# Linear attention and gated MLP layers, prompt kernel: x^T k of the second attention layer by seven block products in place of eight

## The chip, the cores and the metric

The kernel runs on one core of one Trainium2 chip. The metric is the device time of one launch in microseconds (us). Before the change the median of three runs is 1485.83 us (1485.26 to 1486.38). The profile is one execution, with its own time.

## What is computed

The reference applies four blocks to x (2048 tokens of 1024 features): attention, MLP, attention, MLP, each with a layer norm before it and its input added to its output.

```python
def _A_ref(x, wqkv, wo):            # 32 heads of 32
    qkv = (x @ wqkv) ...            # q, k, v per head
    phi = lambda t: jnp.where(t > 0, t + 1, jnp.exp(t)) + 1e-6
    pq, pk = phi(q), phi(k)
    kv = jnp.einsum("bhsd,bhse->bhde", pk, v)
    z = jnp.einsum("bhsd->bhd", pk)
    num = jnp.einsum("bhqd,bhde->bhqe", pq, kv)
    den = jnp.einsum("bhqd,bhd->bhq", pq, z)[..., None] + 1e-6
    return (num / den) ... @ wo

def _B_ref(x, w_gate, w_up, w_down):
    return ((x @ w_gate) * (x @ w_up)) @ w_down
```

## The kernel before, in words

All tokens stay in SBUF as 16 tiles of 128 (X). One program runs layer_A(0), layer_B(1), layer_A(2), layer_B(3). The order of all instructions of each engine is the order in which the program issues them; nothing is reordered later, and each engine takes its own queue in order.

The kernel never forms v. Since kv = pk^T (x wv) = (x^T pk)^T wv, an attention layer computes XK = x^T pk (1024 x 1024) and multiplies it with wv (kv_unit, L662). "x" is here the normed input, xn_a: 16 tiles of 128 tokens x 1024 features, lying in TX, ST and the tails of K6 and K7. The phi-keys are 16 tiles, pk2 in the second layer (f16), in the tails of K0 to K5. The key sums z come from adding the 16 key tiles (sk, f32), splitting the total into two bf16 parts (z_parts, L446: one ScalarE copy, one VectorE subtraction), adding over the tokens with a product with ones (z_unit, L454), and turning the result into a column (z_column, L465).

The second attention layer, where the change is:

- The keys are computed in key_stage (L580), four groups of 512 tokens, each by seven block products for eight (key_product, L546; 8 matmuls of 512 columns each). Group u's products 1, 2, 6, 5, 7 are woven with products 4 and 3 of group u-1. Products 1, 6 and 7 are snapshot from PSUM by ScalarE (key_snap, L556); VectorE adds the snapshots to other products (key_add, L560, the add at L563; block 21 is read by ScalarE at L565). For each of the four blocks (11, 12, 21, 22) there follow exp on ScalarE (key_exp, L569) and three VectorE operations (key_max, L575 and L577). A block 'ln' is token parity l and feature half n. VectorE also forms the block sums of the x operand (key_sums, L534).
- PSUM is eight banks, used as four pairs QP[0] to QP[3]; in this layer key_stage takes them in the order QP3, QP1, QP0, QP2 (R).
- XK in eight pairs (xk_pair, L420): two blocks of 128 rows by 512 columns in one PSUM pair, 16 matmuls each (one for each token tile), and one ScalarE copy to XK (L435). The first pair begins inside key_stage, the last three are spread between the q tiles. XK lies in the heads of K5 and K4, where wk was.
- The key sums: 15 VectorE additions in f32 (sum_unit, L438 to L441), two before product 7 of the last group, two and four in the last round, and the rest while the first pairs run.
- q tiles (q_tile, L472): 16 matmuls (L404), phi by two ScalarE and two VectorE operations (L387, L391, L392, L394), then, some tiles later, through a list that is flushed in twos (L489), the division by the denominator (den_sums, L507; den_divide, L515) and a transposing DMA on SyncE's queue (tx, L340). 11 q tiles stand between the XK pairs, the last five behind kv_unit.
- Queues: SyncE's carries the transposes and the weight loads (load_qkv, L148; wq in the last round of key_stage, wv right behind key_stage). ScalarE's carries wo (load_o, L152). GpSimd's carries, in this stage, only the small norm statistics of tiles 12 to 15 (L296 to L331), woven into the first two rounds (key_norms, L653; KEY_FILL, L651). In the first attention layer GpSimd's queue also issues plain loads (scan_fetch, L223).

Of the kernel before, what the change touches and what calls it, by code (L numbers as in the profile page):

```python
# [38 lines left out]
def kernel(  # L39
# [11 lines left out]
    nc = tc.nc  # L51
    P = 128
# [30 lines left out]
    QQ = psum.tile([P, 8, NB], F32, tag="Q", name="Q")  # L83
    Q = [QQ[:, i, :] for i in range(8)]
    QP = [QQ[:, 2 * i:2 * i + 2, :] for i in range(4)]
    WD = dram.tile([7, P, BLK], F16, name="WD")

    HEAD = KD * NB
# [38 lines left out]
    SS = [K[1][:, i * D:(i + 1) * D].bitcast(F16).rearrange("p (k m s) -> p k m s", k=KH, m=2) for i in range(4)]  # L127
    TK = [W[:, 2 * i * D:2 * (i + 1) * D].bitcast(F16).rearrange("p (k n) -> p k n", n=NB) for i in range(3)]
    yk = [MX[:, i * D:(i + 1) * D].bitcast(F16).rearrange("p (m s) -> p m s", s=NB) for i in range(4)]
    ek = [b[:, i * D:(i + 1) * D].rearrange("p (m s) -> p m s", s=NB) for b in (K[7], K[1]) for i in range(4)]  # L130
    count = {}

    def turn(name, bufs):
        count[name] = count.get(name, -1) + 1
        return bufs[count[name] % len(bufs)]
# [281 lines left out]
            proj_mm(t, wk[n], ps[:, n, :])  # L417
        return ps, pk[t]

    def xk_pair(c, pk, order):  # L420

        n, j = divmod(2 * c, KD)
        bank = []

        def part(ts):
            if not bank:
                bank.append(mm_pair())
            for i in range(2):
                for t in ts:
                    nc.tensor.matmul(out=bank[0][:, i, :], lhsT=xn_a[t][:, (j + i) * P:(j + i + 1) * P],  # L430
                                     rhs=pk[t][:, n * NB:(n + 1) * NB], start=(t == order[0]), stop=(t == order[-1]))

        def end():
            part(order[-2:])
            nc.scalar.copy(out=XK[n][:, j:j + 2, :], in_=bank[0])  # L435
        return [lambda: part(order[:-2]), end]

    def sum_unit(t, eng, pk):  # L438

        def run():  # L440
            eng.tensor_tensor(out=sk, in0=pk[0] if t == 1 else sk, in1=pk[t], op=ALU.add)  # L441
        return run

    zparts = []
# [27 lines left out]
    def q_tile(t, split, mid=[], end=[], ring=4, done=2):  # L472

        while count.get("mm", -1) // 2 + 1 & 3 >= ring:
            mm_pair()
        ps = mm_pair()
        proj_mm(t, wq[0], ps[:, 0, :])
        do(mid)
        proj_mm(t, wq[1], ps[:, 1, :])
        do(end)  # L480
        pq = turn("pq", pqb)
        phi(ps, pq, split)
        for _ in range(done):
            flush()
        later.extend(over_den(t, pq))
# [60 lines left out]
    def key_product(u, p, pair):  # L546
        a11, a12, a21, a22 = key_blocks(u)
        st = {1: a11, 2: a12, 4: a22, 5: SS[0], 6: SS[1], 7: SS[2], 3: SS[3]}[p]
        for m in range(2):
            for k in range(KH):  # L550
                nc.tensor.matmul(out=pair[:, m, :], lhsT=st[:, k, m, :], rhs=kmove[p][:, k, :],  # L551
                                 start=(p in (1, 2, 5) and k == 0), stop=(k == KH - 1), skip_group_check=True)
# [1 line left out]
    kst = {}  # L554

    def key_snap(u, p, bank):  # L556
        kst[u, p] = turn("sk", SK)
        nc.scalar.activation(out=kst[u, p], in_=bank, func=ACT.Identity, bias=kq[:, 1:2])

    def key_add(u, b, sn, bank):  # L560
# [4 lines left out]
            nc.scalar.activation(out=kst[u, b], in_=bank, func=ACT.Identity, bias=kq[:, 1:2])  # L565

    def key_exp(u, b):
        e = turn("ek", ek[:4]) if u < NG - 1 or b == 11 else ek[4 + (22, 21, 12).index(b)]
        nc.scalar.activation(out=e, in_=kst[u, b], func=ACT.Exp, scale=kq[:, 0:1], bias=kq[:, 3:4])  # L569
        kst[u, b] = kst[u, b], e  # L570

# [5 lines left out]
            nc.vector.tensor_tensor(out=pk2[TPG * u + 2 * m + l][:, n * NB:(n + 1) * NB], in0=y[:, m, :],  # L577
                                    in1=e[:, m, :], op=ALU.max)

    def key_stage(R, fill, sks, xk):  # L580

        fill = list(fill)

        def fills(n):
            do(fill[:n])
            del fill[:n]

        fills(3)
        for u in range(NG + 1):
            a, b, c, a_, c_ = R[2 * u % 3], R[3], R[(2 * u + 1) % 3], R[(2 * u - 2) % 3], R[(2 * u - 1) % 3]  # L590
            now, was = u < NG, u > 0
            if now:
                key_product(u, 1, a)
                key_snap(u, 1, a)
            else:
                xk[0][0]()
            if was:
                key_exp(u - 1, 22)
                key_product(u - 1, 4, a_)
                key_add(u - 1, 21, 0, a_)  # L600
                key_exp(u - 1, 21)
                key_max(u - 1, 22)
                fills(KEY_FILL[u][0])
                if not now:
                    do(sks[:2])
                    del sks[:2]
            if now:
                key_product(u, 2, b)
                key_add(u, 11, 1, b)
            if was:  # L610
                key_max(u - 1, 21)
                if now:
                    key_exp(u, 11)
                key_product(u - 1, 3, c_)
# [12 lines left out]
            if now:  # L627
                key_product(u, 5, c)
            if was:
                key_max(u - 1, 12)  # L630
            else:
                key_max(u, 11)
            if not now:
                do(sks[:4])
                del sks[:4]
            if now:
                do(sks[:(0, 0, 0, 2)[u]])
                del sks[:(0, 0, 0, 2)[u]]
                if u == NG - 1:
                    load_qkv(wq, 0)  # L640
                key_product(u, 7, a)
                key_snap(u, 7, a)
                if u + 1 < NG:
                    key_sums(u + 1, (0, 1))
                key_add(u, 22, 7, c)
                if u + 1 < NG:
                    key_sums(u + 1, (2,))
                fills(KEY_FILL[u][2])
        assert not fill

# [177 lines left out]
    def do(units):  # L828
        for u in units:
            u()  # L830
# [32 lines left out]
    SCAN_KEY = tuple(range(4, 12))  # L863

    def layer_A(li, R=None):
        keys = pk2 if li else pk
        sks = [sum_unit(t, nc.vector, keys) for t in range(1, NT)]
        first_A = li == 0
        order = [t for t in range(NT) if t not in (13, 15)] + [13, 15] if li else list(range(NT))
        xk = [xk_pair(c, keys, order) for c in range(KD)]  # L870

        def scans(n=1):
            if first_A:
# [79 lines left out]
        if li:  # L953
            count["mm"] = 1
        rest = [lambda x=x: do(x) for x in xk[first:]]
        XT_ = 11

        for t in range(XT_):
            pos = [-(-len(rest) * x // (XT_ - 1)) for x in (t, t + 1)]
            xks = rest[pos[0]:pos[1]]  # L960
            if t == XT_ - 2:
                do(xks)
                xks = []
                load_o()
            q_tile(t, li > 0, done=2 * ((t > 1 or first_A) and t < XT_ - 1))
            do(xks)
            if t == li // 2:
                z_unit()
            elif t == 2 + li // 2:
                z_column()  # L970
            elif first_A and t == 7:
                scale_sum(0, 2)
            elif first_A and t == 9:
                scale_pow(0, 2)
                scale_root(0, 2)
            elif first_A and t == 10:
# [269 lines left out]
```

## Time and profile before

| what | us |
|---|---|
| median of three runs | 1485.83 |
| the profiled execution's own time | 1486.08 |
| its span | 1484.3 |
| TensorE busy in the span | 1475.9 |
| VectorE busy | 1030.0 |
| ScalarE busy | 739.6 |
| GpSimd busy | 96.5 |
| second layer: first key product to kv product | 750.66 to 894.04 |
| first pair of x^T k to kv product | 796.45 to 894.04 |
| matmuls of x^T k, second layer | 256 |

A line of a timeline reads: start, length, engine, line of the code, operation, output <- input, shape, count; in brackets the idle time before it and who ended it. A line of the chain reads: start, length, what. "L404 x16" is sixteen matmuls of line 404. A matmul's record lasts 0.379 us, but the next one starts 0.216 us after it, so records overlap; VectorE's overlap a little too. A line of a window reads: its limits, its length, then busy time and number of operations of PE, PEld, DVE, ACT and POOL, the granted clock, the share of the DMA engines, and GB/s.

### The profile page before, as it was taken

The numbers are of one execution on the slowest core, as the hardware profiler recorded it, in microseconds if no ns is written. First come the engines' busy times: TensorE is split into PE (matmuls) and PEld (weight loads), VectorE is DVE, ScalarE is ACT, GpSimd is POOL, SyncE is SP. The second block draws the span as 40 slices with busy tenths as digits, with TensorE's granted clock in tenths as the row PEclk, the third lists the DMA queues.
The fourth block names the chain that finished last, engine by engine and source line by source line (L and its number), as shares of the span: only waits on it lengthen the run. The fifth ranks groups of instructions, "written<-read, shape, count | busy, mean of one in ns | idle before, by whom it ended". The sixth has DMA issues, their size and how long they took to land.

```text
span 1484.3 us, 17639 instructions
## 1 busy us (share of the span) xinstructions
PE 1475.9 (99%) x6965; PEld 672.7 (45%) x6965; DVE 1030.0 (69%) x1460; ACT 739.6 (50%) x696; POOL 96.5 (6%) x219
## 2 busy tenths in 40 slices
PE   9999999999999999999999999999999999999999
PEld 3444444444444444444444445444444444444444
DVE  7856788888775577767388567867776846777532
ACT  5887695777601366640185337545663015666200
POOL 2121121000000000001130000200000100000000
PEclk9999999999999999999999999999999999999999
DMA  7867857776656333336533024353332763333442
GB/s 213 202 201 196 252 135 186 210 205 203 214 176 176 85 85 86 88 126 188 174 57 113 16 45 112 70 129 86 86 86 104 235 171 93 86 85 86 154 166 84
DMA packets 269650, 202.73 MB, mean 137 GB/s; under 512 B 101760, under 2 KB 256896, under 8 KB 265984
## 3 DMA queue, kind: packets, MB, share of 16 engines
q1 hardware_dynamic: 261232, 182.61, 43.6%
q0 software_dynamic: 4032, 14.68, 3.0%
q10 hardware_dynamic: 4304, 4.33, 0.9%
q8 instruction: 54, 0.88, 0.2%
q14 instruction: 28, 0.23, 0.0%
HBM read 160.43 MB, written 17.04 MB: 120 GB/s over the span
## 4 chain that ended last, share of the span: by engine, by line
PE 87%; POOL 1%; ACT 0%; DVE 0%; issue 0%
PE Q L755 46%; PE Q L1065 22%; PE Q L689 7%; PE Q L404 5%; PE Q L430 4%; PE Q L551 3%; PE Q L679 0%; PE Q L669 0%; POOL va L329 0%; ACT K L324 0%; POOL rs L330 0%; POOL nm L325 0%; POOL of L331 0%; DVE X L1079 0%; DVE W L396 0%
## 5 line engine op out<-in xcount | busy, mean ns | idle before, releaser
L755 PEld LDWEIGHTS <-K 128*128 128x128 f16 x3136 | 306.8, 98 | 370.0
L755 PE MATMUL Q<-XT,K 128*128 128x512 bf16 (+1 forms) x1792 | 405.7, 379 | 0.0
L1065 PE MATMUL Q<-K,K 128*128 128x512 f16 (+2 forms) x1582 | 340.4, 377 | 0.0
L755 PE MATMUL Q<-TX,K 128*128 128x512 f16 x1344 | 308.4, 379 | 0.0
L717 ACT ACTIVATE K<-K,fac 128x2048 f16<-128x2048 bf16 x112 | 224.6, 2008 | 128.8 <-DMA K<-in_B_w_gate_dram 128.8
L1065 PEld LDWEIGHTS <-K 128*128 128x128 f16 x1582 | 154.3, 98 | 184.5
L720 DVE TENSOR_TENSOR K<-K 128x1024 f16<-128x1024 f16 (+1 forms) x244 | 156.9, 665 | 103.4 <-ACT K L717 101.5
L720 DVE TENSOR_TENSOR W<-MX,Q 128x1024 f16<-128x1024 f32 x88 | 107.3, 1220 | 38.5 <-PE Q L755 19.6
L775 ACT COPY MX<-Q 128x1024 f32<-128x1024 f32 x60 | 60.8, 1012 | 124.1 <-PE Q L755 111.1
L720 DVE TENSOR_TENSOR W<-W,Q 128x1024 f16<-128x1024 f32 x80 | 97.6, 1220 | 17.9 <-PE Q L755 13.6
L775 ACT COPY W<-Q 128x1024 f32<-128x1024 f32 x52 | 52.7, 1013 | 92.2 <-PE Q L755 79.5
L720 DVE TENSOR_TENSOR K<-K,K 128x512 f16<-128x512 f16 (+1 forms) x148 | 87.7, 597 | 4.2
L404 PE MATMUL Q<-K,K 128*128 128x512 bf16 x384 | 86.8, 379 | 1.9 <-DMA K<-K 1.0
L404 PE MATMUL Q<-K,XT 128*128 128x512 bf16 x384 | 85.7, 379 | 1.2 <-DMA XT<-ST 0.6
L759 DVE TENSOR_TENSOR K<-W 128x512 f16<-128x512 f16 x168 | 71.4, 425 | 5.8
L231 ACT ACTIVATE K<-K 128x2048 bf16<-128x2048 bf16 x37 | 70.3, 1906 | 1.6 <-DMA K<-in_B_w_down_dram 1.5
L392 DVE TENSOR_SCALAR W<-W 128x1024 bf16<-128x1024 bf16 (+1 forms) x52 | 20.5, 393 | 66.7 <-ACT W L387 66.6
L1079 DVE SCALAR_TENSOR_TENSOR W<-Q,kap,X 128x1024 f32<-128x1024 f32 x16 | 20.5, 1284 | 66.1 <-PE Q L1065 66.1
L772 ACT COPY MX<-Q 128x1024 f32<-128x1024 f32 x28 | 28.3, 1009 | 71.9 <-PE Q L755 71.9
L387 ACT ACTIVATE W<-Q 128x1024 bf16<-128x1024 f32 (+1 forms) x52 | 49.2, 950 | 29.3 <-PE Q L404 29.3
L290 DVE BATCH_NORM_STATS2 st<-X 128x6 f32<-128x512 bf16 x92 | 58.2, 673 | 2.6 <-DMA X<-in_A_x_dram 2.6
L404 PEld LDWEIGHTS <-K 128*128 128x128 bf16 x384 | 37.2, 98 | 47.4 <-DMA K<-K 2.6
(158 smaller groups left out, 1334.2 us busy)
## 6 DMA issues: line engine op xcount, KB each, us to landing
K<-WD SPq DMA_DIRECT2D x28, 1792.0 KB, 7.5
K<-in_B_w_gate_dram SPq DMA_DIRECT2D x70, 512.0 KB, 4.0
K<-in_B_w_up_dram SPq DMA_DIRECT2D x56, 512.0 KB, 5.2
K<-in_A_wqkv_dram SPq DMA_DIRECT2D x10, 1024.0 KB, 6.0
K<-in_B_w_down_dram POOLq DMA_DIRECT2D x12, 512.0 KB, 5.8
K<-in_B_w_up_dram POOLq DMA_DIRECT2D x11, 512.0 KB, 5.2
K<-in_B_w_down_dram SPq DMA_DIRECT2D x10, 512.0 KB, 5.3
WD<-K SPq DMA_DIRECT2D x10, 512.0 KB, 3.0
```

The source lines that it names most:

```text
L231: nc.scalar.activation(out=scan_buf[i], in_=scan_buf[i], func=ACT.Square, accum_out=acc[:, m, c:c + 1])
L290: nc.vector.bn_stats(out=stat[t][0][:, c, :], in_=X[:, t, c * NB:(c + 1) * NB])
L387: nc.scalar.activation(out=e, in_=ps, func=ACT.Exp)
L404: nc.tensor.matmul(out=ps, lhsT=xt[:, k, tl * P:(tl + 1) * P], rhs=w[:, k, :], start=(k == 0), stop=(k == KD - 1))
L430: nc.tensor.matmul(out=bank[0][:, i, :], lhsT=xn_a[t][:, (j + i) * P:(j + i + 1) * P], rhs=pk[t][:, n * NB:(n + 1) * NB], start=(t == orde ...
L689: nc.tensor.matmul(out=ps[:, n, :], lhsT=xT[t // TPG][:, c, tl * P:(tl + 1) * P].bitcast(F16), rhs=KVo[c][:, n, :], start=(c == 0), stop=( ...
L717: nc.scalar.activation(out=b.bitcast(F16), in_=b, func=ACT.Copy, scale=fac[:, m:m + 1])
L720: eng.tensor_tensor(out=o, in0=a, in1=b, op=op)
L755: nc.tensor.matmul(out=pair[:, m, :], lhsT=stationary(n, p, m, k), rhs=moving[p][:, k, :], start=(p in (1, 2, 5) and k == 0), stop=(k == K ...
L759: nc.vector.tensor_tensor(out=hA[i][:, u, :], in0=gu[:, 0, :], in1=gu[:, 1, :], op=ALU.mult)
L775: nc.scalar.copy(out=snaps[u, p], in_=a)
L1065: nc.tensor.matmul(out=ps_[:, lo:hi], lhsT=act[:, u, j * P:(j + 1) * P], rhs=w[:, u, lo:hi], start=(p in (1, 2, 5) and u == 0), stop=(u == ...
```

## The change

x^T pk of the second layer is seen as 2 x 2 blocks: the tokens by parity of their tile (eight pairs of tiles, 2i and 2i+1), the rows of x^T by feature half, the columns by feature half of the keys. It is computed by seven products of sums of blocks (x_product: for each of two column parts jp, 2 x 8 matmuls of 512 columns). Products 1, 6 and 7 are snapshot from PSUM (SN2), product 4's bank is copied to XK, and products 2, 5 and 3 are added to a snapshot (x_add, VectorE). The sums S (of x, in five operations for eight tile pairs) and T (of the keys, one operation for a pair) are made by VectorE, most of them in place.

The key sums no longer run on VectorE alone. GpSimd's queue copies the first four key tiles into four DRAM rows WZ (f16 to f32; a row of a partition is padded by 64 elements) and adds the next eight to them by accumulating DMAs, a group's four in the round after it. In the last round three more add the four rows into one. VectorE adds the last four tiles (key_total), and one DMA adds the DRAM row to that in SBUF; key_parts takes the place of z_parts. The loop over t in key_stage also runs in the first round, where its range is -4 to 0.

The order of products, sums and q tiles is written out in xq_stage. wv is loaded behind product 6's second part, into the buffers that SX and TY use until then. The buffers of pq are taken by a fixed list in this layer.

```diff
@@ -83,6 +83,7 @@
     QQ = psum.tile([P, 8, NB], F32, tag="Q", name="Q")
     Q = [QQ[:, i, :] for i in range(8)]
     QP = [QQ[:, 2 * i:2 * i + 2, :] for i in range(4)]
+    WZ = [dram.tile([P, D + 64], F32, name=f"WZ{i}")[:, 0:D] for i in range(4)]
     WD = dram.tile([7, P, BLK], F16, name="WD")
 
     HEAD = KD * NB
@@ -127,7 +128,11 @@
     SS = [K[1][:, i * D:(i + 1) * D].bitcast(F16).rearrange("p (k m s) -> p k m s", k=KH, m=2) for i in range(4)]
     TK = [W[:, 2 * i * D:2 * (i + 1) * D].bitcast(F16).rearrange("p (k n) -> p k n", n=NB) for i in range(3)]
     yk = [MX[:, i * D:(i + 1) * D].bitcast(F16).rearrange("p (m s) -> p m s", s=NB) for i in range(4)]
-    ek = [b[:, i * D:(i + 1) * D].rearrange("p (m s) -> p m s", s=NB) for b in (K[7], K[1]) for i in range(4)]
+    ek = [b[:, i * D:(i + 1) * D].rearrange("p (m s) -> p m s", s=NB) for b in (K[7], K[1], MX) for i in range(4)]
+    SX, TY = (K[i][:, 0:HEAD].bitcast(F16).rearrange("p (i n) -> p i n", n=NB) for i in (3, 1))
+    SN2 = [b.bitcast(F32).rearrange("p (m s) -> p m s", s=NB)
+           for b in (K[0][:, HEAD:HEAD + 2 * D], MX[:, 2 * D:4 * D], W[:, 0:2 * D], W[:, 2 * D:4 * D], K[4][:, 0:2 * D])]
+    sk2, zhi, zlo = MX[:, 2 * D:4 * D].bitcast(F32), W[:, 5 * D:6 * D], MX[:, D:2 * D]
     count = {}
 
     def turn(name, bufs):
...
@@ -554,7 +559,7 @@
     kst = {}
 
     def key_snap(u, p, bank):
-        kst[u, p] = turn("sk", SK)
+        kst[u, p] = SN2[0] if (u, p) == (NG - 1, 6) else turn("sk", SK)
         nc.scalar.activation(out=kst[u, p], in_=bank, func=ACT.Identity, bias=kq[:, 1:2])
 
     def key_add(u, b, sn, bank):
@@ -565,7 +570,7 @@
             nc.scalar.activation(out=kst[u, b], in_=bank, func=ACT.Identity, bias=kq[:, 1:2])
 
     def key_exp(u, b):
-        e = turn("ek", ek[:4]) if u < NG - 1 or b == 11 else ek[4 + (22, 21, 12).index(b)]
+        e = turn("ek", ek[:4]) if u < NG - 1 or b == 11 else ek[{22: 4, 21: 8, 12: 9}[b]]
         nc.scalar.activation(out=e, in_=kst[u, b], func=ACT.Exp, scale=kq[:, 0:1], bias=kq[:, 3:4])
         kst[u, b] = kst[u, b], e
 
@@ -577,7 +582,7 @@
             nc.vector.tensor_tensor(out=pk2[TPG * u + 2 * m + l][:, n * NB:(n + 1) * NB], in0=y[:, m, :],
                                     in1=e[:, m, :], op=ALU.max)
 
-    def key_stage(R, fill, sks, xk):
+    def key_stage(R, fill, xp):
 
         fill = list(fill)
 
@@ -592,18 +597,20 @@
             if now:
                 key_product(u, 1, a)
                 key_snap(u, 1, a)
-            else:
-                xk[0][0]()
             if was:
                 key_exp(u - 1, 22)
+                if not now:
+                    xp(1, 0, QP[0])
+                    xp(1, 1, QP[2])
                 key_product(u - 1, 4, a_)
                 key_add(u - 1, 21, 0, a_)
                 key_exp(u - 1, 21)
                 key_max(u - 1, 22)
                 fills(KEY_FILL[u][0])
                 if not now:
-                    do(sks[:2])
-                    del sks[:2]
+                    xsums("S2", XG)
+                    tsums("T2", range(4))
+                    tsums_last((4, 5), 1)
             if now:
                 key_product(u, 2, b)
                 key_add(u, 11, 1, b)
@@ -626,17 +633,16 @@
             fills(KEY_FILL[u][1])
             if now:
                 key_product(u, 5, c)
-            if was:
+            if was and now:
                 key_max(u - 1, 12)
-            else:
+            elif now:
                 key_max(u, 11)
-            if not now:
-                do(sks[:4])
-                del sks[:4]
             if now:
-                do(sks[:(0, 0, 0, 2)[u]])
-                del sks[:(0, 0, 0, 2)[u]]
+                for t in range(TPG * (u - 1), TPG * u if was else 0):
+                    nc.gpsimd.dma_start(out=WZ[t % 4], in_=pk2[t], **({"accum_op": ALU.add} if t > 3 else {}))
                 if u == NG - 1:
+                    for i, j in ((0, 1), (2, 3), (0, 2)):
+                        nc.gpsimd.dma_start(out=WZ[i], in_=WZ[j], accum_op=ALU.add)
                     load_qkv(wq, 0)
                 key_product(u, 7, a)
                 key_snap(u, 7, a)
@@ -645,6 +651,10 @@
                 key_add(u, 22, 7, c)
                 if u + 1 < NG:
                     key_sums(u + 1, (2,))
+                if u > 1:
+                    tsums("T3", range(2 * u - 4, 2 * u - 2))
+                if u:
+                    xsums("S3", XG[(0, 0, 1, 3)[u]:(0, 1, 3, 5)[u]])
                 fills(KEY_FILL[u][2])
         assert not fill
 
+    def xpart(i, l, h, n=1):
+        return [xn_a[2 * j + l][:, h * NB:(h + 1) * NB] for j in range(i, i + n)]
+    def xspan(i, l, h, n):
+        if n == 1:
+            return xpart(i, l, h)[0]
+        b = TX[:, 0:6 * D] if i == 0 else ST[:, 0:4 * D]
+        return b.rearrange("p (i l h s) -> p i l h s", l=2, h=2, s=NB)[:, :, l, h, :]
+    XG = ((0, 3), (3, 2), (5, 1), (6, 1), (7, 1))
+    def xsums(which, groups):
+        for i, n in groups:
+            a11, a12, a21, a22 = (xspan(i, l, h, n) for h, l in ((0, 0), (0, 1), (1, 0), (1, 1)))
+            s2 = SX[:, i:i + n, :] if n > 1 else SX[:, i, :]
+            o, a, b, op = {"S3": (a21.bitcast(F16), a11, a21, ALU.subtract), "S2": (s2, a22, a21.bitcast(F16), ALU.subtract),
+                           "S1": (a11.bitcast(F16), s2, a11, ALU.add), "S4": (a12.bitcast(F16), a12, s2, ALU.subtract)}[which]
+            nc.vector.tensor_tensor(out=o, in0=a, in1=b, op=op)
+    def tsums(which, pairs):
+        for i in pairs:
+            b11, b21, b12, b22 = (pk2[2 * i + l][:, n * NB:(n + 1) * NB] for n in range(2) for l in range(2))
+            t2 = TY[:, i, :]
+            o, a, b, op = {"T3": (b12, b22, b12, ALU.subtract), "T2": (t2, b12, b11, ALU.add),
+                           "T1": (b11, b22, t2, ALU.subtract), "T4": (b21, b21, t2, ALU.subtract)}[which]
+            nc.vector.tensor_tensor(out=o, in0=a, in1=b, op=op)
+    def tsums_last(pairs, at):
+        for i in pairs:
+            b11, b21, b12, b22 = (pk2[2 * i + l][:, n * NB:(n + 1) * NB] for n in range(2) for l in range(2))
+            t = MX[:, (2 * at + i % 2) * NB:(2 * at + i % 2 + 1) * NB].bitcast(F16)
+            nc.vector.tensor_tensor(out=t, in0=b12, in1=b11, op=ALU.subtract)
+            nc.vector.tensor_tensor(out=TY[:, i, :], in0=b22, in1=t, op=ALU.subtract)
+    xsnap = {}
+    def x_product(p, jp, pair):
+        def operands(i, c):
+            even, odd = xn_a[2 * i], xn_a[2 * i + 1]
+            ke, ko = pk2[2 * i], pk2[2 * i + 1]
+            st = {1: even, 2: odd, 4: odd[:, NB:], 6: SX[:, i, :], 5: even.bitcast(F16), 7: even[:, NB:].bitcast(F16),
+                  3: odd.bitcast(F16)}[p]
+            mv = {1: ke[:, 0:NB], 2: ko[:, 0:NB], 3: ko[:, NB:], 4: ko[:, 0:NB], 6: TY[:, i, :], 5: ke[:, 0:NB], 7: ke[:, NB:]}[p]
+            return st[:, c * P:(c + 1) * P], mv
+        for pairs in (range(6), range(6, 8)):
+            for m in range(2):
+                for i in pairs:
+                    st, mv = operands(i, 2 * jp + m)
+                    nc.tensor.matmul(out=pair[:, m, :], lhsT=st, rhs=mv, start=(p in (1, 2, 5) and i == 0),
+                                     stop=(i == 7), skip_group_check=True)
+        if p in (1, 6, 7):
+            xsnap[p, jp] = SN2[{1: 2 + jp, 6: 0, 7: 4 - 3 * jp}[p]]
+            nc.scalar.copy(out=xsnap[p, jp], in_=pair)
+        elif p == 4:
+            nc.scalar.copy(out=XK[0][:, KH + 2 * jp:KH + 2 * jp + 2, :], in_=pair)
+    def x_add(p, jp, pair):
+        n, c, sn = {2: (0, 0, 1), 5: (1, KH, 7), 3: (1, 0, 6)}[p]
+        nc.vector.tensor_tensor(out=XK[n][:, c + 2 * jp:c + 2 * jp + 2, :], in0=xsnap.pop((sn, jp)), in1=pair, op=ALU.add)
+    def key_total():
+        nc.vector.tensor_tensor(out=sk2, in0=pk2[12], in1=pk2[13], op=ALU.add)
+        for t in (14, 15):
+            nc.vector.tensor_tensor(out=sk2, in0=sk2, in1=pk2[t], op=ALU.add)
+        nc.gpsimd.dma_start(out=sk2, in_=WZ[0], accum_op=ALU.add)
+    def key_parts():
+        nc.scalar.copy(out=zhi, in_=sk2)
+        nc.vector.tensor_tensor(out=zlo, in0=sk2, in1=zhi, op=ALU.subtract)
+        zparts[:] = [zhi, zlo]
+    def at_pair(i):
+        count["mm"] = 2 * i - 1
+    def xq_stage():
+        def q(t, i, done):
+            at_pair(i)
+            q_tile(t, True, done=done)
+        x_product(2, 0, QP[3])
+        x_product(2, 1, QP[1])
+        x_add(2, 0, QP[3])
+        key_max(NG - 1, 12)
+        tsums_last((6, 7), 0)
+        x_add(2, 1, QP[1])
+        x_product(6, 0, QP[0])
+        key_total()
+        tsums("T3", (4, 5, 6, 7))
+        q(0, 1, 0)
+        x_product(7, 0, QP[0])
+        xsums("S1", XG)
+        tsums("T1", range(8))
+        q(1, 3, 0)
+        x_product(5, 0, QP[1])
+        tsums("T4", range(8))
+        key_parts()
+        x_add(5, 0, QP[1])
+        q(2, 3, 0)
+        x_product(4, 0, QP[0])
+        xsums("S4", XG)
+        at_pair(3)
+        z_unit()
+        x_product(3, 0, QP[1])
+        x_add(3, 0, QP[1])
+        q(3, 3, 4)
+        x_product(6, 1, QP[2])
+        load_qkv(wv, 2)
+        at_pair(0)
+        z_column()
+        q(4, 1, 2)
+        x_product(7, 1, QP[2])
+        q(5, 3, 2)
+        x_product(5, 1, QP[0])
+        x_add(5, 1, QP[0])
+        q(6, 1, 2)
+        x_product(4, 1, QP[2])
+        q(7, 3, 2)
+        x_product(3, 1, QP[0])
+        x_add(3, 1, QP[0])
+        load_o()
+        q(8, 1, 2)
+        q(9, 0, 2)
+        q(10, 2, 0)
+        at_pair(3)
...
             count["mm"] = 7
-            key_stage(R, key_norms(), sks, xk)
-            load_qkv(wv, 2)
-            count["mm"] = 5
+            key_stage(R, key_norms(), x_product)
             eps[0] = kq[:, 2:3]
-        first = 3 if first_A else 2
+            xq_stage()
+        first = 3 if first_A else 0
         for i in range(first):
-            if first_A:
-                do(xk[i])
-            elif i == 0:
-                do([xk[1][0], xk[0][1]])
-            else:
-                do(xk[1][1:])
-            do(sks[5 * i:5 * i + 5] if first_A or i == 0 else sks[5 * i:])
...
-        for t in range(XT_):
+        for t in range(XT_ if first_A else 0):
...
         kv_unit()
+        if not first_A:
+            at_pair(1)
```

More of the change, by code (lines that the diff above doesn't have):

```diff
@@ L418, in k_tile, with xk_pair @@
         return ps, pk[t]
-    def xk_pair(c, pk, order):
+    def xk_pair(c):
         n, j = divmod(2 * c, KD)
@@ L430, in part, with sum_unit @@
                     nc.tensor.matmul(out=bank[0][:, i, :], lhsT=xn_a[t][:, (j + i) * P:(j + i + 1) * P],
-                                     rhs=pk[t][:, n * NB:(n + 1) * NB], start=(t == order[0]), stop=(t == order[-1]))
+                                     rhs=pk[t][:, n * NB:(n + 1) * NB], start=(t == 0), stop=(t == NT - 1))
         def end():
-            part(order[-2:])
+            part(range(NT - 2, NT))
             nc.scalar.copy(out=XK[n][:, j:j + 2, :], in_=bank[0])
-        return [lambda: part(order[:-2]), end]
-    def sum_unit(t, eng, pk):
+        return [lambda: part(range(NT - 2)), end]
+    def sum_unit(t):
         def run():
-            eng.tensor_tensor(out=sk, in0=pk[0] if t == 1 else sk, in1=pk[t], op=ALU.add)
+            nc.vector.tensor_tensor(out=sk, in0=pk[0] if t == 1 else sk, in1=pk[t], op=ALU.add)
         return run
@@ L480, in q_tile @@
         do(end)
-        pq = turn("pq", pqb)
+        pq = turn("pq", pqb) if eps[0] == 1e-6 else pqb[t % 4 if t < 6 else (4, 5, 0, 1, 2, 3)[t % 6]]
         phi(ps, pq, split)
@@ L865, in layer_A @@
     def layer_A(li, R=None):
-        keys = pk2 if li else pk
-        sks = [sum_unit(t, nc.vector, keys) for t in range(1, NT)]
+        sks = [sum_unit(t) for t in range(1, NT)]
         first_A = li == 0
-        order = [t for t in range(NT) if t not in (13, 15)] + [13, 15] if li else list(range(NT))
-        xk = [xk_pair(c, keys, order) for c in range(KD)]
+        xk = [xk_pair(c) for c in range(KD)]
         def scans(n=1):
@@ L935, in layer_A @@
             count["mm"] = 7
-            key_stage(R, key_norms(), sks, xk)
-            load_qkv(wv, 2)
-            count["mm"] = 5
+            key_stage(R, key_norms(), x_product)
             eps[0] = kq[:, 2:3]
-        first = 3 if first_A else 2
+            xq_stage()
+        first = 3 if first_A else 0
         for i in range(first):
-            if first_A:
-                do(xk[i])
-            elif i == 0:
-                do([xk[1][0], xk[0][1]])
-            else:
-                do(xk[1][1:])
-            do(sks[5 * i:5 * i + 5] if first_A or i == 0 else sks[5 * i:])
+            do(xk[i])
+            do(sks[5 * i:5 * i + 5])
             if i == first - 1:
@@ L952, in layer_A @@
             scans(3)
-        if li:
-            count["mm"] = 1
         rest = [lambda x=x: do(x) for x in xk[first:]]
         XT_ = 11
-        for t in range(XT_):
+        for t in range(XT_ if first_A else 0):
             pos = [-(-len(rest) * x // (XT_ - 1)) for x in (t, t + 1)]
@@ L964, in layer_A @@
                 load_o()
-            q_tile(t, li > 0, done=2 * ((t > 1 or first_A) and t < XT_ - 1))
+            q_tile(t, False, done=2 * (t < XT_ - 1))
             do(xks)
-            if t == li // 2:
+            if t == 0:
                 z_unit()
-            elif t == 2 + li // 2:
+            elif t == 2:
                 z_column()
-            elif first_A and t == 7:
+            elif t == 7:
                 scale_sum(0, 2)
-            elif first_A and t == 9:
+            elif t == 9:
                 scale_pow(0, 2)
                 scale_root(0, 2)
-            elif first_A and t == 10:
+            elif t == 10:
                 scale_bits(0, 2)
```

## Prediction

> **What bounds the kernel now.** I read the chain that ended last first, then its pieces in order of time, then TensorE's waits.
>
> ```profile
> ## 4 chain that ended last, share of the span: by engine, by line
> PE 87%; POOL 1%; ACT 0%; DVE 0%; issue 0%
> ...
> ```
>
> ```profile
> 754.85 41.60 PE Q L551 x192
> 796.45 6.04 PE Q L430 x28
> 802.49 3.45 PE Q L551 x16
> 805.95 7.77 PE Q L430 x36
> 813.72 3.45 PE Q L404 x16
> ...
> 894.21 3.57 PE Q L669 x64
> ```
>
> ```profile
> PE Q L551 <- ACT K L558: 0.6, 1, 0.6
> ```
>
> TensorE carries the end, and from 754.85 us, through the second layer's key stage and x^T k to the kv product, it never stops: the one wait of the key stage (0.6 us) ends where that chain begins. So a matmul removed here is worth its whole pitch, as long as no operand or bank comes late. Then VectorE, ScalarE and the GpSimd issues, because they get the new work:
>
> ```profile
> 788.55 0.55 DVE L575 TENSOR_SCALAR K<-K,fac,kq 128x1024 bf16<-128x1024 bf16 x1 [0.71 <-ACT K L569]
> 789.13 0.76 DVE L577 TENSOR_TENSOR K<-MX,K 128x512 f16<-128x512 f16 x2
> 789.81 1.21 DVE L563 TENSOR_TENSOR MX<-W,Q 128x1024 f16<-128x1024 f32 x1
> ...
> 811.78 13.82 DVE L441 TENSOR_TENSOR K<-K,K 128x1024 f32<-128x1024 f32 x11
> ```
>
> ```profile
> 754.00:796.00 42.00, 41.43 (x193) 18.67 (x191) 36.84 (x65) 34.78 (x33) 4.46 (x11) 1.00 0.17 36
> 796.00:894.00 98.00, 98.00 (x463) 44.51 (x461) 62.06 (x81) 35.88 (x35) 0.00 (x0) 1.00 0.26 74
> ```
>
> ```profile
> q0 software_dynamic: 4032, 14.68, 3.0%
> ```
>
> ```profile
> L223 POOL DMA_DIRECT2D K<-in_B_w_up_dram x11: 748/748/971, 87.3 to 120.0; - x11
> ...
> DMA to landing us min/median/max: 3.7/5.1/10.7
> ```
>
> In the two stretches (columns: busy time of PE, PEld, DVE, ACT, POOL) VectorE is busy 88% and 63%, ScalarE 83% and 37%, GpSimd idle in the second.
>
> **What is removed from the path.** In the chain 768 matmuls of 512 columns take 165.76 us: 0.2158 us each, granted clock 1.00. x^T k was 8 pairs x 32 = 256 matmuls, 55.2 us; seven products x 2 x 16 = 224 take 48.3 us. Gain 32 x 0.2158 = 6.9 us. Mixed f16/bf16 operands change nothing: L551 runs such pairs at the same 0.379 us record. The eight PSUM copies on ScalarE (L435, 1.01 us) become six snapshots and two copies at the same price.
>
> **VectorE.** Removed: 15 f32 key sums, 1.256 us apart in the chain, 18.8 us. Added, at the spacing of the nearest rows: 36 f16 sums of 512 columns, 28 of them 0.34 us apart (two L577 take 0.76 with their 0.42 overlapped) and the 8 in dependent pairs 0.40; four sets of x sums, each one of 1536 columns (0.87 us, my estimate between L534's 0.60 for 1024 and L544's 1.13 for 2048), one of 1024 (0.60), three of 512 (0.34), 2.5 us a set; six PSUM adds like L563, 1.13; three f32 sums, 1.256. That is 9.5 + 3.2 + 10.0 + 6.8 + 3.8 = 33.3 us, net +14.5 on 98.9, in a stretch that falls from 140 to 133 us: 85% busy. It fits on average; the order decides. I walked each queue in order on the old clock, TensorE without gaps: products 1 at 796.3 and 799.7, key products 4 and 3 at 803.2 and 804.9, product 2 at 806.6 and 810.1, 6 at 813.5, q(0) 817.0, 7 at 820.5, q(1) 823.9, 5 at 827.4, q(2) 830.8, 4 at 834.3, z 837.7, 3 at 838.6, and so on to the kv product at 887.3.
> - Key stage, third round: T3 and S3 add 0.68 + 0.94 us in front of L575; 0.71 of idle takes part, so L563 (789.81) comes about 0.9 late. Behind it on ScalarE stands exp of block 11, and behind that the snapshot that key product 7 (794.6) awaits: 0 to 0.3 us of stall.
> - Product 2's second half needs bank QP1 at 810.1. VectorE from 797.7: add 1.13, T3+S3 1.36, max 1.25, S2 2.5, T2 1.4, last pairs 1.6 = 806.9; block 21's exp ends 807.4; max 1.25, add 1.13 = 809.8. Slack 0.3.
> - Product 5 (827.4) needs S1 and T1: add 811.4, max 812.7, pairs 814.3, add 815.4, key_total 819.2, T3 820.5; then phi of q(0) is first in the queue and waits for q(0) and two ScalarE operations, to 823.25; S1 825.7; T1 one by one, the sixth at 827.8, due 828.5. Slack 0.7.
> - Products 4 and 3: T4 is done at 832.9 (due 834.3); S4's first sums at 837.9 and 838.5 (due 838.6 and 839.2). After that VectorE is as loaded as before: four plus six times two flushes equal the former eight times two, and the later adds have over 3 us.
>
> If every sum cost its full record (0.42, 0.68, 0.95) instead of its spacing, these places would lose 0.4 + 0.7 + 0.3 = 1.4 us. If all holds, nothing; no gain beyond 6.9 is possible, since TensorE did not wait here. Walked the same way, the old order comes out 0.3 us earlier than its trace, which about uses up the slack of the first two places: I take 0.4 us.
>
> **Moved loads.** Wv (2 MB) goes from about 797 to behind product 6's second half (849) and the two transposes of q(0) and q(1) on SP's queue; landing near 861, it is wanted at 887. 26 us of matmuls cover it; uncovered it would cost 5 to 8. Wo is wanted 19 us after its issue and takes 8.4 at most. Nothing for either. In the first round the new loop's range is -4 to 0: four copies of stale tiles stand on GpSimd's queue before tile 13's variance (762.8); 4 x 0.75 us more and ScalarE still wants its offset only at 773.
>
> **The key sums' DMA chain.** The trace has no accumulating or casting DMA; the nearest row is a plain GpSimd transfer of 512 KB: issue 0.75 us, landing 5.1 (3.7 to 10.7). The chain begins when the third group's keys are complete (797.8): four accumulations, two sums of two rows, one sum, and one into SBUF. Each link waits on GpSimd for the landing before it; nothing else is queued behind. Seven issues in series, 797.8 + 7 x 0.75 = 803.05, plus four landings L. What waits at the end is the copy of the total (zhi) on ScalarE, from 829.5, and behind it phi of q(2) and, on VectorE, zlo; z at 837.7 is delayed once the total lands after 834.7. So L may be (834.7 - 803.05) / 4 = 7.9 us. At 5.1 the total waits for key_total instead (819.2) and lands at 825. An accumulation also reads its destination: one such transfer held the 16 engines 0.030 x 1484.3 / 28 = 1.6 us, so doubling that makes L 6.7, the total at 830: still nothing. I take 6.7, the row plus the extra read. At 10.7 the total lands at 845.9 and the loss is 11.2 plus 1.5 (phi, S4 and product 3 line up behind) = 12.7. The keys' T3 in place must also wait for these DMAs: the tightest pair at 798.9, its transfer issued by 787.5, so L up to 11.4 is free. A gain is excluded, as nothing of this was on the path.
>
> Here a rule speaks against the change. The Trainium skill, SBUF — State Buffer, section "SBUF: two separate sides", has it that a DMA issued from GpSimd needs descriptors which GpSimd can't write while VectorE holds the shared port; its section "A bandwidth-pool intuition that's wrong" gives 3.1 us instead of 0.62 for one beside a copy. The 28 issues in this trace took 0.70 to 0.97 us, but VectorE was less busy there than the 85% here; and GpSimd's tiny L325, 0.2 us else, took 1.27 beside one VectorE operation. By the rule's figure seven issues take 21.7, the total lands at 819.5 + 20.4 = 839.9, loss 5.2 + 1.5: the gain is gone. By the row it is nothing, and even a wait of one whole VectorE operation (1.22) per issue gives 832. I go by the row.
>
> **Sum.** Span 1484.3 - 6.9 + 0.4 = 1477.8. The profiled execution took 1486.08, 1.78 around its span; the median of the three runs is 1485.83, 0.25 below it: 1485.83 - 6.5 = 1479.3.
>
> **Rivals.** (A) As summed, 1478.9 to 1479.9: chance 0.62. For it: TensorE's unbroken chain and VectorE's slack. (B) VectorE becomes the bound at products 2, 5 and 3, at full records or with ScalarE's hand-overs added: 1.4 to 3 us lost, 1480.3 to 1482: 0.17. For it: slacks of 0.3 to 0.7 us; against: most new sums are independent and lie back to back. (C) The DMA chain ends late: from L = 7.9 it eats the gain, 4 us per us of L; at 9.2 the gain is gone, at 10.7 it gives 1485.83 - 6.9 + 12.7 = 1491.6, slower than before. For it: four dependent landings, unmeasured work in the engines, the rule above; against: the median row, and wv's 2 MB leave that stretch. Chance 0.18: faster 0.04, no change 0.05, slower 0.09. (D) The 32 matmuls go, but lost time elsewhere in the layer (kv product, transposes) gives it all back, 1485.8: 0.03.
>
> A change of 0.2% (3.0 us) is about what a measurement of this kernel can tell from none. Faster: 0.62 + 0.17 + 0.04 = 0.83; within: 0.05 + 0.03 = 0.08; slower: 0.09. Range 1478.2 to 1483.3: below it nothing but noise, above it most of C and D, under 0.2.
>
> **What would show it.** 224 matmuls in x^T k and the kv product near 887.3 or earlier: A. TensorE waiting for VectorE's sums at products 2, 5 or 3: B. ScalarE's zhi waiting past 834.7 for the last accumulation, and z behind it: C; landings under 7.9 us refute it. If no wait is seen on TensorE and the kv product has not moved by 6 us, the count is wrong.

## The result, and the profile after

The changed kernel takes 1479.00 us (median of six runs, 1478.43 to 1479.45); before, 1485.74 (six runs). The ratio is 0.9954, with a 95% interval of 0.9941 to 0.9967: 6.8 us faster, against 6.5 forecast. The profiled execution's span is 1477.3 us, before 1484.3.

Line numbers have moved: x_product's matmuls are L725, the q tiles L409 (L404 before), the kv product L810, kvo_unit (the product of kv with wo) L820, the output tiles L830; the VectorE sums are L692 (x), L700 and L706/L707 (keys), the adds to snapshots L735. TensorE's waits in the whole kernel that concern this layer (columns: total, times, longest):

```profile
PE Q L556 <- ACT K L563: 0.6, 1, 0.6
...
PE Q L820 <- DVE W L812: 0.2, 1, 0.2
```

The first is the old wait at the layer's first product. The second is new, and it lies behind the kv product, where the forecast had no place for one. The chain that ended last now breaks there:

```profile
895.93 0.01 DVE W L397
895.94 0.04 issue
895.98 0.38 PE Q L820
```

The chain is followed back from the end of the kernel, on TensorE but for its last 0.4 us, to 895.98; ahead of that it stands on VectorE's queue. So its shares (PE 39%) don't mean that TensorE had become idle; they say that the first gap met on the way back is this one. The windows that answer to the two shown before (busy PE, PEld, DVE, ACT, POOL, then clock, DMA share, GB/s):

```profile
754.00:796.00 42.00, 41.76 (x193) 18.90 (x193) 38.48 (x69) 34.19 (x33) 11.76 (x21) 1.00 0.72 178
796.00:887.30 91.30, 91.30 (x440) 41.83 (x439) 70.51 (x120) 36.61 (x36) 6.92 (x8) 1.00 0.53 132
```

VectorE is busy 92% and 77% (88% and 63% before), TensorE without a gap behind that old wait; the DMA share rises from 0.17 and 0.26 to 0.72 and 0.53.

Since the start of the stage varies between profiles (its first product begins at 749.5 to 751.5 us in the changed kernel and its variants), I measure the change in the stage itself, between starts of TensorE's groups. The x^T k product and the kv product, before and after, in the timeline (the chain shown ahead, with 796.45, starts a row where the one before it ends):

```profile
796.29 1.46 PE L430 MATMUL Q<-K,TX 128*128 128x512 f16 x6
...
894.04 3.74 PE L669 MATMUL Q<-K,K 128*128 128x128 bf16 x64
```

```profile
795.81 0.81 PE L725 MATMUL Q<-K,TX 128*128 128x512 f16 x3
...
886.68 3.74 PE L810 MATMUL Q<-K,K 128*128 128x128 bf16 x64
```

| stage, us | before | after |
|---|---|---|
| first key product to first x^T k product | 45.63 | 45.75 |
| first x^T k product to kv product | 97.75 | 90.87 |
| kv product to first output tile | 24.30 | 24.63 |
| output tiles | 55.25 | 55.25 |

The second row gives 6.88 of the 6.91 us that 32 matmuls are worth. The first loses 0.12, the third 0.33, so the layer as a whole gains 6.43. The two spans differ by 7.0; the other 0.6 lies ahead of the layer, which starts at 750.66 us before and at 750.06 after, where the kernels do the same work. I take it for variation between executions and not for a gain of the change.

GpSimd's DMA chain, and what waits for its end on ScalarE:

```profile
797.21 3.51 POOL L642 DMA_DIRECT2D WZ<-K  x4 [8.96 <-DVE K L582]
807.54 0.88 POOL L645 DMA_DIRECT2D WZ<-WZ  x1 [6.82 <-DMA WZ<-K]
812.07 0.81 POOL L645 DMA_DIRECT2D WZ<-WZ  x1 [3.64 <-DMA WZ<-K]
817.92 0.81 POOL L645 DMA_DIRECT2D WZ<-WZ  x1 [5.04 <-DMA WZ<-WZ]
824.07 0.91 POOL L741 DMA_DIRECT2D MX<-WZ  x1 [5.33 <-DVE TX L692]
```

```profile
WZ<-K POOLq DMA_DIRECT2D x16, 512.0 KB, 6.4
...
WZ<-WZ POOLq DMA_DIRECT2D x3, 512.0 KB, 5.5
MX<-WZ POOLq DMA_DIRECT2D x1, 512.0 KB, 5.4
```

```profile
829.53 1.05 ACT L744 CAST W<-MX 128x1024 bf16<-128x1024 f32 x1 [0.39 <-DMA MX<-WZ]
```

A landing is counted from the start of its issue: 824.07 + 5.4 is where ScalarE starts. Each issue stands behind the landings that it needs: the first two sums behind those of the rows, the third behind both of these, the last behind the third. At 824.07 the profile names a VectorE operation, but VectorE's part of the total ended at 818.66; what came last is the third sum's landing (817.92 + 5.5 = 823.4), with the issue 0.6 us behind it. The total lands at 829.5, where I had it at 830 (829.5 on this profile's clock, which is 0.5 us ahead); z would be late from 834.2.

### The profile page after: what moved, and what is told of

Same layout as the page of the kernel before. It is cut to its first block, busy times and chain, and to the rows that moved or that the text cites. A ratio compares the mean times of both kernels' runs of the same rounds, so it can differ in the third digit from the quotient of the medians.

```text
span 1477.3 us, 17671 instructions
## 1 busy us (share of the span) xinstructions
PE 1468.1 (99%) x6933; PEld 669.2 (45%) x6933; DVE 1044.1 (71%) x1510; ACT 740.1 (50%) x696; POOL 111.2 (8%) x239
## 5 line engine op out<-in xcount | busy, mean ns | idle before, releaser
L409 PE MATMUL Q<-K,K 128*128 128x512 bf16 x384 | 87.0, 379 | 1.9 <-DMA K<-K 1.6
L409 PE MATMUL Q<-K,XT 128*128 128x512 bf16 x384 | 86.0, 379 | 0.6 <-ACT XT L379 0.4
L301 POOL TENSOR_SCALAR ve<-mv 128x1 f32<-128x1 f32 x45 | 11.3, 251 | 720.1 <-DVE mv L299 719.6
L409 PEld LDWEIGHTS <-K 128*128 128x128 bf16 x384 | 37.1, 98 | 48.0 <-DMA K<-K 3.6
```

What stands on the lines that cost most here:

```text
L409: nc.tensor.matmul(out=ps, lhsT=xt[:, k, tl * P:(tl + 1) * P], rhs=w[:, k, :], start=(k == 0), stop=(k == KD - 1))
```

## The experiments

Each is measured against runs of the kernel before on the same chip. "Over the changed kernel" is (ratio - 0.9954) x 1486 us. The stage length is that from the first x^T k product to the kv product (90.87 in the changed kernel).

**e1, the sums back on VectorE**

```diff
-  ... GpSimd's DMAs to WZ, among its rows, and from WZ[0] to sk2
+  for t in range(1, 12):                  # last round, ahead of S2
+      nc.vector.tensor_tensor(out=sk4, in0=pk2[0] if t == 1 else sk4, in1=pk2[t], op=ALU.add)
+  tsums("T3", range(4))
```

> The DMA chain undone, the block products kept: VectorE makes the sums of tiles 0 to 11 itself (11 more f32 adds in the last round, and one more in key_total), T3 of the first four pairs behind them. My theory: VectorE's order had 0.0 us of slack at product 2 and 0.5 at product 5, so what is added there goes to TensorE: 11 x 1.256 + 0.7 for the T3 that moves in at product 2, and 1.256 - 0.5 at product 5, in all 15 us: 1494. Rival, VectorE's idle share of 15 to 20% swallows the sums: 1479 to 1480, and the DMA chain was not needed.

Measured: 1495.06 us, ratio 1.0060 (1.0046 to 1.0073), 15.8 over the changed kernel, and slower than before. Its wait of TensorE:

```profile
PE Q L722 <- DVE K L582: 13.7, 1, 13.7
```

The stage is 106.80, 15.9 longer: 13.7 of wait, and 2.2 since the granted clock was 0.50 to 0.63 in the 8 us around the restart (at 822.71):

```profile
812.00:816.00 4.00, 0.00 (x0) 0.00 (x0) 3.93 (x7) 0.00 (x0) 0.00 (x0) 0.67 0.00 0
...
824.00:828.00 4.00, 4.00 (x13) 1.49 (x12) 3.44 (x8) 1.24 (x1) 0.00 (x0) 0.63 0.00 0
```

So VectorE's idle share does not swallow the sums: without the DMA chain, the block products as ordered here would be a loss. The eleven adds stand in one place here, in the last round ahead of S2; whether they would fit if spread over the stage was not tried.

**e2, no DMA chain**

```diff
-  nc.gpsimd.dma_start(...)                # all with WZ
```

> All DMAs to and from the padded rows are left out; the total is that of the last four key tiles only (part of the key sums is left out). My theory: the chain lies wholly beside TensorE's work, so the time stays that of the changed kernel, 1479.0 within 0.4; only the transposes of tiles 12 to 15 land sooner. Rival, the DMAs cost something through contention or through VectorE's waits for them: 0.5 to 2 us faster, 1477 to 1478.5.

Measured: 1479.37 us, ratio 0.9954 (0.9941 to 0.9966); stage 90.87. The chain costs nothing that can be measured. The transposes of tiles 12 to 15 take 6.8 us to land beside it (median), and 3.2 without it: they are slowed, but TensorE loses nothing by it.

**e3 and e4, one and two links more**

```diff
+  nc.gpsimd.dma_start(out=WZ[1], in_=WZ[0])     # e3; e4 also WZ[2] from WZ[1]
-  nc.gpsimd.dma_start(out=sk2, in_=WZ[0], accum_op=ALU.add)
+  nc.gpsimd.dma_start(out=sk2, in_=WZ[1], accum_op=ALU.add)     # e4: WZ[2]
```

> One more link in the chain: the summed row is copied to another row, and that is added to the total in SBUF. In the changed kernel the total landed at 829.5 on its profile's clock; z is delayed from 834.2 on. My theory: one link is 0.8 + 5.4 us and a short wait, the total lands near 835.5, z waits 1.3 and product 3 some 1.5 behind it: 1479.0 + 2.8 = 1481.8. Rival, the total's landing is not near the path, since z could wait longer unseen: 1479.0.

> Two more links in the chain. My theory: the total lands near 841.7, z waits 7.5 us and product 3 1.5 behind it: 1479.0 + 9.0 = 1488.0, slower than before. Rival, the landing is not near the path: 1479.0. Between this and one link the slope should be one link per link, 6.2 us.

Measured: e3 1481.61 us, ratio 0.9968 (0.9957 to 0.9980), 2.1 over the changed kernel, stage 92.90; e4 1487.59 us, ratio 1.0009 (1.0002 to 1.0016), 8.2 over it, stage 99.35. When the total came, in e3 and e4:

```profile
835.35 1.04 ACT L745 CAST W<-MX 128x1024 bf16<-128x1024 f32 x1 [5.51 <-DMA MX<-WZ]
```

```profile
841.14 1.04 ACT L746 CAST W<-MX 128x1024 bf16<-128x1024 f32 x1 [11.17 <-DMA MX<-WZ]
```

and TensorE's waits in e4:

```profile
PE Q L464 <- ACT W L396: 5.9, 1, 5.9
PE Q L727 <- DVE TX L694: 0.6, 1, 0.6
```

In e3 z waits 0.2 us and product 3 1.4 behind it; with e3's clock 0.7 us behind the changed kernel's, the total came just past the forecast threshold (834.9 there). In e4 z waits for phi of q(2), which stands behind zhi on ScalarE, as forecast. Its sum is forecast well (9.0) but made up differently: 6.5 of waits, and 2.0 because the clock fell to 0.50 and the matmuls after the gap (at 844.16) ran at half speed (stage 8.5 longer):

```profile
841.00:843.00 2.00, 0.00 (x0) 0.00 (x0) 0.78 (x1) 1.86 (x2) 0.00 (x0) 0.61 0.00 0
...
847.00:849.00 2.00, 2.00 (x8) 0.80 (x7) 1.18 (x4) 0.08 (x1) 0.00 (x0) 0.68 0.00 0
```

The waits are less than forecast since, with the clocks lined up at the first x^T k product, the added link took 5.1 us in e3 and the next one 5.7 in e4, not 6.2; that the sum still agrees is luck. What the two runs show is the time behind which a landing of the total is paid for; the rival, that the landing is off the path, is refuted.

**e5 and e10, the 32 matmuls put back; e9, another order of pq buffers**

```diff
+  x_product(2, 0, QP[3])                  # e5, e10: each half of product 2 twice
+  x_product(2, 1, QP[1])
-  pqb[t % 4 if t < 6 else (4, 5, 0, 1, 2, 3)[t % 6]]
+  pqb[t % 4 if t < 6 else (4, 5, 2, 3, 0, 1)[t % 6]]             # e9, e10
```

> Product 2's two halves are each computed twice (the second starts the bank anew), 32 matmuls more, the number of before. My theory, a matmul on the unbroken chain is worth its 0.2158 us: 1479.0 + 6.9 = 1485.9, the time of before. Rival, some of the gain came from elsewhere (the moved load of wv, fewer VectorE sums): 1483 to 1485.

Measured: 1488.22 us, ratio 1.0014 (1.0007 to 1.0020), 8.9 over the changed kernel, more than either theory had. The stage is 97.76, just 6.89 longer, so the matmuls cost their pitch; the excess lies behind: kv product to output tile takes 26.12 where it was 24.63. (The profiled execution took 1487.41; no profile shows where the median's further 0.8 us lie.) VectorE and TensorE there:

```profile
893.36 0.69 DVE L399 TENSOR_TENSOR W<-W 128x1024 bf16<-128x1024 bf16 x1 [5.04 <-DMA XT<-W]
```

```profile
PE Q L822 <- DVE W L814: 1.5, 2, 1.3
```

q(8)'s phi writes the buffer from which q(4)'s transpose still reads; that transpose was issued when the 2 MB of wo were loading, and took 9.4 us to land (in the changed kernel 7.9, where the transposes around it took 3.1 to 3.3). Everything behind it on VectorE is late, the mask products of the kv product (L814) last. The same in the changed kernel, smaller, and the mask products behind it:

```profile
885.00 0.69 DVE L399 TENSOR_TENSOR W<-W 128x1024 bf16<-128x1024 bf16 x1 [3.54 <-DMA XT<-W]
...
894.65 1.28 DVE L812 TENSOR_TENSOR W<-Q,mask 128x512 bf16<-128x512 f32 x2
```

> Only the fixed list of pq buffers changes: q(8) and q(9) take the buffers of q(2) and q(3), whose transposes are long done, and q(10) and q(11) those of q(4) and q(5). In the changed kernel VectorE waited 3.5 us at q(8) for q(4)'s transpose, which the load of wo slows, and the mask products of the kv product came 0.2 us late for TensorE. My theory: both waits go, 0.0 to 0.3 us faster than the changed kernel, 1478.7 to 1479.0. Rival, the lateness comes from VectorE's load and not from that buffer: the same waits remain.

> The kernel with 32 more matmuls, with the new order of pq buffers. That kernel came 8.7 us above the changed one and not 6.9; its profile shows VectorE waiting 5.0 us at q(8) for q(4)'s transpose and TensorE 1.3 us for the mask products behind it. My theory: with the buffer free, the excess goes and what is left is the matmuls: the changed kernel plus 6.9, ratio to before 1.000. Rival, a matmul more costs more than its pitch: the ratio stays near 1.0014.

Measured: e9 1478.76 us, ratio 0.9948 (0.9936 to 0.9961). Its interval overlaps the changed kernel's, so the time alone does not separate them; the profile does: the mask products start some 3 us earlier,

```profile
891.90 1.28 DVE L812 TENSOR_TENSOR W<-Q,mask 128x512 bf16<-128x512 f32 x2
```

TensorE does not wait at kvo_unit, and the kv product is 24.29 us ahead of the output tiles, where it was 24.63 (24.30 before). By its profile e9 is the best version here, by some 0.3 us. e10 1486.62 us, ratio 1.0001 (0.9993 to 1.0010): stage 97.76 and 24.29 behind it, both those of the kernel before (97.75 and 24.30). The transposes beside the wo load take just as long there (9.3 us), so it is the buffer that made them matter. With 256 matmuls the time is the old one, so the rest of the change, taken together, did not move it (by more than 1.0 us down or 1.5 up, the interval).

**e6 and e11, more work ahead of product 5**

```diff
+  for _ in range(8):                      # e11: 4
+      nc.vector.tensor_tensor(out=MX[:, D:2 * D].bitcast(F16), in0=pk2[12], in1=pk2[13], op=ALU.add)
   xsums("S1", XG)
```

> Eight idle f16 adds of 1024 columns (0.60 us each, 4.8 in all) stand on VectorE ahead of S1, before product 5. My theory: the slack there is 0.5 us, so TensorE waits 4.3 us at product 5: 1483.3. Rival, product 5 does not bind and VectorE makes the time up in its waits for phi: 1479.0 to 1479.5.

> Four idle adds ahead of S1 (2.4 us) where eight were. With eight, TensorE waited 4.4 us and its granted clock then fell to 0.5 for about 3.5 us, so that 6 to 7 us were lost. My theory: the wait is 4.4 - 2.4 = 2.0 us, too short for the clock to fall, so the loss over the changed kernel is 2.0 and no more. Rival, any such wait lowers the clock, or the excess with eight had another source: 2.7 us or more.

Measured: e6 1486.18 us, ratio 1.0000 (0.9991 to 1.0008), 6.8 over the changed kernel; e11 1481.39 us, ratio 0.9967 (0.9954 to 0.9979), 1.9 over it. e6's restart after its wait, in TensorE's timeline, and the windows of 2 us around it:

```profile
824.66 2.54 PE L409 MATMUL Q<-K,XT 128*128 128x512 bf16 x11
831.64 1.46 PE L725 MATMUL Q<-K,TX 128*128 128x512 f16 x3 [4.44 <-DVE K L700]
```

```profile
828.00:830.00 2.00, 0.00 (x0) 0.00 (x0) 1.97 (x4) 1.39 (x3) 0.00 (x0) 1.00 0.60 117
830.00:832.00 2.00, 0.36 (x1) 0.13 (x2) 2.00 (x7) 0.92 (x1) 0.00 (x0) 0.72 0.00 0
832.00:834.00 2.00, 2.00 (x6) 0.76 (x5) 2.00 (x7) 0.00 (x0) 0.00 (x0) 0.50 0.00 0
834.00:836.00 2.00, 2.00 (x10) 0.87 (x9) 1.90 (x6) 0.00 (x0) 0.00 (x0) 0.93 0.01 4
```

The wait is the forecast one (4.3, measured 4.4), so product 5's slack of about 0.5 us is right. But 6 matmuls from 832 to 834, where 10 run from 834 to 836, show the second cost, the clock. If it is either 1.00 or 0.50 within a window, the mean of 0.72 puts its fall at 830.9, and that of 0.93 its return at 834.3: it falls 3.7 us after TensorE's last matmul (which ends at 827.2), and returns 2.7 us after it resumes. Worked out the same way, it fell after 3.2 us and returned after 4.1 in e4, and after 4.3 and 4.2 in e1. Matmuls at half speed for 2.7 us lose 1.3 us by that, and the stage is 5.9 longer where the wait is 4.4. In e11:

```profile
PE Q L725 <- DVE K L700: 1.5, 1, 1.5
```

the clock stays at 1.00 in every window of 2 us from 824 to 836, and the stage is 2.3 longer (the rest are short pauses between the next matmuls). The Trainium skill's page TensorE: Matmul & The Clock Gate ("Part 1: The HAM clock gate") gives about 3.4 us of idleness for that drop and about as much activity for the return. The rows lie around that, 3.2 to 4.3 us for the drop and 2.7 to 4.2 for the return; 3.4 us at half speed would cost an estimated 1.7 us, where the stage lost 1.5 in e6, 2.0 in e4 and 2.2 in e1 on top of the waits. e6's median is another 1.2 us above its profile (1485.0), and no profile shows where.

**e7, a pitch of 8 KB**

```diff
-  WZ = [dram.tile([P, D + 64], F32, ...
+  WZ = [dram.tile([P, 2 * D], F32, ...
```

> The padding of the DRAM rows goes from 64 to 1024 elements, so that the rows lie 8192 bytes apart where they lay 4352. My theory: the landings stay within the chain's slack of 4.7 us, the time stays 1479.0. Rival, the pitch sets the speed of the accumulation, landings of 7 us and more, and z waits: 1481 or more.

Measured: 1479.47 us, ratio 0.9954 (0.9940 to 0.9969), stage 90.88. The sums between rows land in 6.7 us in place of 5.5 (medians of three; 5.4 to 5.9 in the other runs with the old pitch), and zhi waits 2.5 us in place of 0.4; the chain's slack covers it. So in this profile the pitch acts on the landing, and not on the time.

**e8, without the first round's copies**

```diff
-  for t in range(TPG * (u - 1), TPG * u if was else 0):
+  for t in range(TPG * (u - 1), TPG * u) if was else ():
```

> The four copies of stale tiles in the first round are left out; the result needs none of them. My theory: they cost nothing, since tile 13's offset is wanted 8 us later: 1479.0 within 0.4. Rival, their 2 MB delay the transposes of tiles 12 to 15, or GpSimd's statistics behind them, enough to reach TensorE: up to 0.5 us faster.

Measured: 1479.02 us, ratio 0.9951 (0.9936 to 0.9966), stage 90.88. They cost nothing that can be measured; the transposes still take 6.7 us, so it is the second round's copies that slow them.

## Why the prediction was right, point by point

- *32 matmuls at 0.2158 us.* Right: 6.88 in the stage, and e10 puts the old time back on top of e9 with the matmuls alone.
- *VectorE's load and order.* Its sum was forecast at 113.4 us busy or 85%; between 754 and 887 it is 108.7, or 82%, in part because work of q(8) and later, held up by the 3.5 us below, falls behind 887 (in e9 it is 111.4). The places with the least slack were right: at the third round TensorE lost 0.12 (0 to 0.3 forecast), at product 2 nothing with 0.0 left, at product 5 nothing with 0.5 left (0.7 forecast). e6 and e11 show that slack's end, e1 that of product 2.
- *0.4 us lost.* The size is right, 0.45, but by luck, as most of it (0.33) lay elsewhere. The step "after that VectorE is as loaded as before ... the later adds have over 3 us" failed: it counted VectorE's work and left out the buffers. With the fixed list, q(8) waits for q(4)'s transpose (3.5 us) and the mask products come late. "Nothing for either" was too short for wo: its load is in time, but that transpose takes 7.9 us beside it in place of some 3.2. e9 and e10 show what the buffer costs.
- *The DMA chain.* L was taken as 6.7. The landings were 6.4 in the median for keys to rows, up to 12.7 among four issued together, and then 5.5 and 5.4. So the forecast chain was too quick at its start, where four transfers run together, and too slow in its single links: the second sum was issued at 812.1 instead of 807.0 (on this clock), and the three links from there took 17.5 us instead of 22.4. That these cancelled, and the total came when forecast, is luck. The threshold and the place of the loss were right (e3, e4). One term of rival C was missing: a gap of more than some 3 to 4 us also lowers the clock.
- *The rule against the change.* By it, seven issues were to take 21.7 us and undo the gain. The groups of four took 2.2 to 3.6 us and the single ones 0.81 to 0.91, with VectorE busy 99% from 797 to 801 and 96% from 807 to 820, where the first seven of the chain's issues stand. The longest record was 1.9, the last of an accumulating group. The rule's stall did not appear in the issues (whether a landing holds some of it was not separated). But the Trainium skill's page SBUF — State Buffer ("SBUF: two separate sides") ties the stall to VectorE operations in a 2-port mode, such as an f32 copy, and VectorE's work beside these issues was mostly tensor_tensor: the prediction took the rule more widely than it is stated, and these runs do not test its 3.1 us. Its sums were also mixed, with landings of 5.1 there and 6.7 above; with 6.7, a wait of one VectorE operation per issue would have put the total at 838.4 and not 832, behind the threshold.
- *Moved loads and stale copies.* Nothing, as forecast (e8 for the copies; for wv the stage's length, with no wait at the kv product).

## What to carry to other kernels

Where one engine runs without a gap, the gain of removing its work is its pitch times the count, and the whole question is whether the work added elsewhere keeps each operand and bank on time: walk each queue in order and look for the place with the least slack, since an average busy share (here 82%) says little when 5 us at the wrong place cost 6.8. Walk the buffers as well as the operations: who still reads the one that is written next, a DMA above all. And price a stall of TensorE that is longer than some 3 to 4 us higher than its length: here 4.4 us cost 5.9, and 1.5 left the clock alone.

## What was not expected of the hardware

- TensorE's granted clock fell to 0.50 between 3.2 and 4.3 us after the last matmul (e4, e6, e1), and in e1 it stayed there for 13.6 us of gap and restart; the half-speed matmuls cost 1.5 to 2.2 us on top of waits of 4.4 to 13.7.
- Four accumulating transfers of 512 KB, issued together beside a 2 MB load, took up to 12.7 us to land (what the accumulation and what the load did to that was not separated); single ones took 5.4 to 5.5, little more than the plain 5.1, and 7.2 where the last of the four were still landing.
- Transposing DMAs beside this traffic took 6.8 us in place of 3.2, and beside the wo load 7.4 to 9.4.
